# A retention and two routed layers: the state's product in 64x64 parts, tile shapes grouped, first and small slots in another order

## Chip, cores and metric

One core of a Trainium2 chip runs the whole program. The metric is the device time of one launch in microseconds; the time before is the median of three runs. Lower is better.

## What is computed

The reference, cut to what matters (B = 4, H = 8, S = 768, D = 64; N = B S = 3072 tokens of 512 elements; 8 experts, F = 1024):

```python
for t in range(S):                                  # retention
    state = gamma * state + einsum('bhd,bhe->bhde', k[:, :, t], v[:, :, t])
    y[:, :, t] = scale * einsum('bhd,bhde->bhe', q[:, :, t], state)
x = y.transpose(0, 2, 1, 3).reshape(B * S, H * D)
# layer 1: one expert per token
logits = x @ w_gate + modality_bias[modality_id]
e = argmax(logits); gate_w = softmax(logits)[e]
x[mask_e] = gate_w * (relu(x[mask_e] @ w1[e]) @ w2[e])
# layer 2: the same without the bias, and times sigmoid(x @ w_output_gate)[e]
```

All is in 32-bit floats. The layers' products split each operand into a high and a low part (names ending in h and l, as w1h and w1l), of which three products are summed.

## The kernel before

**Retention** (0 to 154.6 us). A unit is one batch's chunk of 128 tokens with all eight heads: 24 units, six chunks for each of four batches. For a unit, q and k, with a decay put on by POOL (`scale`: sq, sv), are turned to have the head's elements on partitions (`tr`: four 128x128 transposes, ACT copies the result to qT or kT), then come the scores q k (`scores`, L651, in two banks, heads of odd and even number apart), which DVE masks into P (L655), and `attend`: the state's product Z q (L664, block diagonal Z of two heads, 128x128, only where the chunk isn't a batch's first) and the values' product P sv (L669) are summed in one bank, from which ACT copies yT (L671). `update` adds k sv to the state (L681, in po[0]); DVE copies one half of it to Z (L684), ACT the other (L685), into tiles whose other blocks POOL zeroed once.

One unit later `rows` turns yT back (L577) so that a row holds a token, and computes the routing's partial products with the gate's weights wgp in four 32-column tiles (L581; DVE copies them to yl, L583); `logits` sums these (L587). Groups of tokens then go through `choose` (L183 to L207, with an exponential rex on ACT, L197), `rank` (L215 and L217, matmuls that count tokens of each expert), `place` and `weigh`; a token's row is then scattered to its expert's block of x1d by an indirect DMA on POOL. Rows that nobody fills are `blank`ed by copies of zeros on SP's queue, in units 3 to 6. After unit 17 `decide` names the first expert, whose weights are fetched behind it.

**Layers.** The rows of an expert are worked through in slots: 256 rows (`run`) or, for the rest, up to 128 (`run_small`). A slot fetches rows (xqb), turns them on DVE (`xpose`, L540), splits them (`xsplit`: xh on ACT L545, xl on DVE L547), multiplies with w1 (L892 or the same in `mm1s`), applies relu and splits (hh, hl), and multiplies with w2 (L910). `split1` and `split2` make the high halves of w1 and w2 on ACT (L505, L510) and the low ones on POOL or DVE (L506, L511). While a slot runs, the layer's outputs (ob) are turned and routed for the next layer (`route`, oT, `tr`, `lgm`, `rank`), at steps listed in BIG_AT, SMALL_AT and FIRST_AT. Layer 1 ends at about 499 us, layer 2 at about 835.

**What sets the order.** Each engine runs its instructions in the order in which the program is written; no scheduler moves them. PE, DVE, ACT, POOL and SP wait for one another by semaphores, so an instruction that waits holds up all behind it on its engine. In the retention the loop over units writes the order: fetch, scale, transposes of the next unit's k, scores, transposes of the next q, rows and logits of the last unit, attend, update, and the lists `early` and `late` of routing steps before and behind attend.

## Time and profile before

| | us |
|---|---|
| median of three runs | 842.93 (841.94 to 845.92) |
| the profiled execution | 841.21 |
| its span | 839.4 |
| PE busy in the span | 796.4 (95%) |
| DVE, ACT, POOL busy | 430.2, 276.4, 192.5 |

The mean granted clock of TensorE is 0.994 of its full rate. The durations below come from the profiled execution: a row gives the start, the busy time, the engine, the line and the tiles, and in brackets for how long the engine had stood idle and what released it. Busy times of neighbours on PE overlap, so the length of a block is the difference of two starts.

### The profile page before, as it was taken

The page shows a single profiled execution, that of the slowest core. Times are in us where ns is not written, and L with a number is a line of the kernel's source. Part 1 is how long each engine was busy: PE and PEld are TensorE (multiplying, and loading weights), DVE is VectorE, ACT ScalarE, POOL GpSimd, SP SyncE. Part 2 cuts the span into 40 slices and gives each one's busy share as a digit, 9 for nine tenths or more (in the row PEclk, how much of TensorE's full clock was granted, in tenths as well). Part 3 has the DMA queues.
Part 4 walks back from the last instruction along what each step waited for, and adds up shares of the span by engine and source line. Part 5 has one row for each costly group of instructions (what it writes and reads, how often), then busy time and mean ns, then how long its engine had stood idle before and what let it go on. Part 6 is the DMA issues. An engine that isn't in the chain of part 4 may idle for free. (4 is left out here: it accounts for less than half of the span.)

```text
span 839.4 us, 18443 instructions
## 1 busy us (share of the span) xinstructions
PE 796.4 (95%) x5987; PEld 691.8 (82%) x5987; DVE 430.2 (51%) x1110; ACT 276.4 (33%) x476; POOL 192.5 (23%) x291
## 2 busy tenths in 40 slices
PE   8999998899999997999999968989999999999996
PEld 8788877878899876888998757887899799999794
DVE  4544565754443338444443586223736485463762
ACT  3444445411221216212212532112424362332641
POOL 3455464811110012111001214011111111011111
PEclk9999999999999999999999999999999999999999
DMA  9988799464111124411221531622636277171531
GB/s 168 229 229 195 161 234 264 176 205 119 37 49 28 39 55 144 139 46 37 74 51 42 167 127 29 232 62 53 189 95 210 75 244 237 51 236 45 183 103 40
DMA packets 149688, 106.98 MB, mean 127 GB/s; under 512 B 94845, under 2 KB 125693, under 8 KB 149504
## 3 DMA queue, kind: packets, MB, share of 16 engines
q1 hardware_dynamic: 141664, 85.37, 38.0%
q0 software_dynamic: 6400, 18.98, 6.1%
q8 instruction: 73, 1.20, 0.6%
q14 instruction: 111, 0.91, 0.4%
q10 hardware_dynamic: 1440, 0.53, 0.3%
HBM read 167.64 MB, written 25.83 MB: 230 GB/s over the span
## 5 line engine op out<-in xcount | busy, mean ns | idle before, releaser
L892 PE MATMUL hT<-xh,w1h 128*128 128x256 f32 x768 | 221.2, 288 | 5.2 <-ACT xh L545 3.0
L892 PE MATMUL hT<-xl,w1h 128*128 128x256 f32 x768 | 215.5, 281 | 2.7 <-DVE xl L547 2.0
L892 PE MATMUL hT<-xh,w1l 128*128 128x256 f32 x768 | 215.0, 280 | 0.0
L910 PE MATMUL po<-w2h,hh 128*128 128x512 f32 x432 | 172.3, 399 | 0.3
L910 PE MATMUL po<-w2l,hh 128*128 128x512 f32 x432 | 171.2, 396 | 0.0
L892 PEld LDWEIGHTS hT<-xh,w1h 128*128 128x128 f32 x768 | 144.9, 189 | 14.0 <-issue 7.6
L892 PEld LDWEIGHTS hT<-xl,w1h 128*128 128x128 f32 x768 | 145.1, 189 | 4.7 <-DVE xl L547 3.2
L892 PEld LDWEIGHTS hT<-xh,w1l 128*128 128x128 f32 x768 | 144.8, 188 | 0.0
L910 PE MATMUL po<-w2h,hl 128*128 128x512 f32 x432 | 136.4, 397 | 1.6 <-DVE hl L884 1.1
L884 DVE SCALAR_TENSOR_TENSOR hl<-hT,hh 128x512 fp32r<-128x512 f32 x96 | 65.2, 689 | 129.6 <-ACT hh L883 99.2
L883 ACT ACTIVATE hh<-hT 128x512 fp32r<-128x512 f32 x96 | 57.0, 597 | 192.9 <-PE hT L892 171.9
L910 PEld LDWEIGHTS po<-w2h,hl 128*128 128x128 f32 x432 | 81.0, 188 | 23.1 <-DVE hl L905 2.0
L910 PEld LDWEIGHTS po<-w2h,hh 128*128 128x128 f32 x432 | 81.4, 188 | 19.7 <-ACT hh L904 1.6
L910 PEld LDWEIGHTS po<-w2l,hh 128*128 128x128 f32 x432 | 81.4, 188 | 18.1
L469 POOL DMA_INDIRECT x2d<-ob,r_idx x28 | 29.6, 1057 | 243.4 <-DVE ob L260 105.2
L920 POOL DMA_INDIRECT out_dram<-ob,to x28 | 29.9, 1069 | 187.0 <-DVE ob L918 135.6
L545 ACT ACTIVATE xh<-xTb 128x512 fp32r<-128x512 f32 x58 | 33.5, 624 | 99.3 <-DVE xTb L540 87.7
L511 DVE TENSOR_TENSOR w2l<-raw,w2h 128x1024 fp32r<-128x1024 f32 x40 | 47.3, 1233 | 14.2 <-DMA xqb<-x1d 6.7
L506 DVE TENSOR_TENSOR w1l<-raw,w1h 128x512 fp32r<-128x512 f32 x80 | 49.8, 684 | 2.5 <-ACT w1h L505 2.5
L547 DVE TENSOR_TENSOR xl<-xTb,xh 128x512 fp32r<-128x512 f32 x58 | 37.5, 688 | 22.3 <-ACT xh L545 22.3
L540 DVE STREAM_TRANSPOSE xTb<-xqb 128x1024 f32<-128x1024 f32 x29 | 36.0, 1242 | 24.4 <-DMA xmb<-x2d 13.4
L505 ACT ACTIVATE w1h<-raw 128x512 fp32r<-128x512 f32 (+1 forms) x84 | 47.7, 640 | 0.0
(205 smaller groups left out, 969.0 us busy)
## 6 DMA issues: line engine op xcount, KB each, us to landing
raw<-in_w_dram SPq DMA_DIRECT2D x248, 512.0 KB
xqb<-x2d SPq DMA_DIRECT2D x124, 64.0 KB
xqb<-x1d SPq DMA_DIRECT2D x108, 64.0 KB
nq<-in_q_dram SPq DMA_DIRECT2D x24, 256.0 KB
nk<-in_k_dram SPq DMA_DIRECT2D x24, 256.0 KB
nv<-in_v_dram SPq DMA_DIRECT2D x24, 256.0 KB
x1d<-zrow SPq DMA_DIRECT2D x4, 516.0 KB
x2d<-zrow SPq DMA_DIRECT2D x4, 516.0 KB
```

The lines of the kernel that those rows point to most:

```text
L469: return nc.gpsimd.indirect_dma_start(out=dst, out_offset=bass.IndirectOffsetOnAxis(ap=rp.idx[:, t:t + 1], axis=0), in_=row, in_offset=Non ...
L505: nc.scalar.activation(w1h[i][:, cols], raw1[i][:, cols], AF.Copy)
L506: los[i].tensor_tensor(w1l[i][:, cols], raw1[i][:, cols], w1h[i][:, cols], op=ALU.subtract)
L511: los[i].tensor_tensor(w2l[i], raw2[i], w2h[i], op=ALU.subtract)
L540: nc.vector.transpose(xT.rearrange("p k (a i) -> p a k i", i=32), xq.rearrange("p a (k i) -> p a k i", k=KD))
L545: nc.scalar.activation(hi[:, k:k + 2, :], xT[:, k:k + 2, :], AF.Copy)
L547: nc.vector.tensor_tensor(lo[:, k:k + 2, :], xT[:, k:k + 2, :], hi[:, k:k + 2, :], op=ALU.subtract)
L883: nc.scalar.activation(hh[b], hT[b], AF.Relu)
L884: nc.vector.scalar_tensor_tensor(hl[b], in0=hT[b], scalar=0.0, in1=hh[b], op0=ALU.max, op1=ALU.subtract)
L892: nc.tensor.matmul(to, lhsT=a[k][:, fs], rhs=b[:, k, :], start=(k == 0 and m == 0), stop=(k == KD - 1 and m == 2))
L910: nc.tensor.matmul(po[h], lhsT=x[b][:, o:o + P], rhs=w[f // 2][:, f % 2, :], start=(f == 0 and i == 0), stop=(f == KF - 1 and x is hl))
L920: nc.gpsimd.indirect_dma_start(out=out, out_offset=bass.IndirectOffsetOnAxis(ap=to[:, t:t + 1], axis=0), in_=o[:, :DM], in_offset=None, bo ...
```

## The change

1. `attend` multiplies with the state in eight 64x64 products instead of four block-diagonal 128x128 ones. The output lies in two banks (hT[3] and xT), the halves of which ACT and DVE copy to yT. Z is one 128x256 tile that DVE copies alone; POOL's zeroed tiles are gone. `rows` permutes its transposes to match, and the gate's weights are loaded in four parts on ACT's queue.
2. In the loop over units products of one tile shape stand together: scores, routing parts (now `parts`, in 128 columns of the bank of the small results), transposes of the next q, rows, transposes of the next k (in the scores' first bank), logits, the routing steps, attend, update. The `late` steps stand before attend. w1's low half is made by DVE, not POOL, behind update in units 20 to 22.
3. The blank rows are written in unit 22, behind the first expert's weights, and no scatter waits for them.
4. In a layer's first slot DVE makes all of w2's low half, at other steps; in small slots of layer 1 each step of split2 stands one later, split1's second half stands behind the output, and SMALL_AT has later steps.

The diff, cut to its core:

```diff
-            if i == 1:
-                rows(0)
-            elif 1 < i < n - 1:
-                tr(i + 1, "kT", "k")
             scores(i)
-            if i == 1:
-                tr(2, "kT", "k", po[1])
+            mask(i, 0)
+            if i:
+                parts(i - 1)
+            mask(i, 1)
             if 0 < i < n - 1:
                 tr(i + 1, "qT", "sq")
-            if i > 1:
+            if i:
                 rows(i - 1)
+            if 0 < i < n - 1:
+                tr(i + 1, "kT", "k", pS[0])
+            if i:
+                logits(i - 1)
             if i == n - 1:
                 xsplit(xh, xl, xTf, "h")
-            if n - 4 <= i < n - 1:
-                split1([nc.gpsimd] * KD, [i - n + 4] if i < n - 2 else [2, 3])
-            if 2 < i < 7:
-                blanks.append(blank(x1d, 2 * i - 6))
-                if i == 6:
-                    blanks.append(blank0(x1d))
+            if i == n - 2:
+                blanks.extend([blank(x1d, e) for e in range(0, E, 2)] + [blank0(x1d)])
             for f in early.get(i, []):
                 f()
+            run(*[f() for f in late.get(i, [])])
-            attend(i, lambda: logits(i - 1) if i else None)
+            attend(i)
             update(i)
+            if n - 4 <= i < n - 1:
+                split1([nc.vector] * KD, [i - n + 4] if i < n - 2 else [2, 3])
-            run(*[f() for f in late.get(i, [])])
...
             if c:
+                for s in range(2):
+                    for r in range(2):
+                        for h in range(2):
+                            o = slice(r * D, r * D + D)
+                            nc.tensor.matmul(py[r][h * D:(h + 1) * D, s, :], lhsT=st["Z"][o, 2 * h + s, :], rhs=d["qT"][o, 2 * h + s, :],
+                                             start=(s == 0), stop=False, skip_group_check=True)
...
-            nc.scalar.activation(yT[i % 2], py, AF.Copy)
+                if r:
+                    nc.vector.tensor_copy(yT[i % 2][:, 2:], py[r])
+                else:
+                    nc.scalar.activation(yT[i % 2][:, :2], py[r], AF.Copy)
...
-                        split2([nc.gpsimd] * 2 + [nc.vector] * 2, ({0: (2, 0, 1), 1: (3,)}, {1: (2, 0), 2: (1, 3)})[self.li - 1].get(f, ()))
+                        split2([nc.vector] * 4, ({0: (0,), 3: (1,), 5: (2,), 7: (3,)}, {1: (0,), 2: (1,), 5: (2,), 7: (3,)})[self.li - 1].get(f, ()))
...
-                self.split2((0,) if self.li == 1 else (0, 1), los)
+                if self.li == 2:
+                    self.split2((0, 1), los)
-                        self.split2((((1,), (2, 3), ()), ((), (2,), (3,)))[self.li - 1][j - 1], los)
+                        self.split2((((0,), (1,), (2, 3)), ((), (2,), (3,)))[self.li - 1][j - 1], los)
-                        self.split1(1)
                 self.done(1)
+                self.split1(1)
-        BIG_AT, SMALL_AT, FIRST_AT = (1, 3, 4, 7, 7, 16, 1), (1, 2, 3, 4, 4, 8, 0), (1, 2, 4, 6, 6, 8, 0)
+        BIG_AT, SMALL_AT, FIRST_AT = (1, 3, 4, 7, 7, 16, 1), (1, 2, 4, 6, 6, 8, 0), (1, 2, 4, 6, 6, 8, 0)
```

What the change moves on PE in a steady unit. Before, from the last of the eight scores, which the transposes of the next k (L638, nk) stand ahead of, to the values' product:

```order
L651 MATMUL hT2_118<-qT_1066,kT_1048 128x128
L638 MATMUL hT0_116<-ident_68,sq_1040 128x128 x4
L577 MATMUL po1_121<-ident_68,yT0_136 128x128 x4
L581 MATMUL xT_122<-yT0_136,wgp_74 32x128 x4
L664 MATMUL hT3_119<-qT_1066,Z0_138 128x128 x4
L587 MATMUL misc_123<-cst_67,yl0_137 128x8
L669 MATMUL hT3_119<-P0_1130,sv_954 64x128
L669 MATMUL hT3_119<-P1_1132,sv_954 64x128
```

After, the same part of a unit:

```order
L652 MATMUL hT2_118<-qT_1321,kT_1332 128x128
L585 MATMUL misc_123<-yT1_124,wgp_74 32x128 x4
L639 MATMUL hT0_116<-ident_68,sq_1296 128x128 x4
L578 MATMUL po1_121<-ident_68,yT1_124 128x2x64 x4
L639 MATMUL hT1_117<-ident_68,nk_1214 128x128 x4
L591 MATMUL misc_123<-cst_67,yl1_125 128x8
L671 MATMUL hT3_119<-qT_1321,Z_1378 64x128 x2
L671 MATMUL xT_122<-qT_1321,Z_1378 64x128 x2
L671 MATMUL hT3_119<-qT_1321,Z_1378 64x128 x2
L671 MATMUL xT_122<-qT_1321,Z_1378 64x128 x2
L676 MATMUL hT3_119<-P0_1401,sv_1222 64x128 x4
L676 MATMUL xT_122<-P1_1408,sv_1222 64x128 x4
```

The transposes of k moved from before the scores to between rows and logits, the routing parts to just behind the scores, and the logits out of the attention; the state's product has eight rows of 64 columns in place of four of 128.

On DVE at the end of the retention (units 21 to 23), before, from the copy of logits and the transposition of the first slot's rows (L540) to the last unit's masks (L655):

```order
L588 COPY r1_lg_238<-misc_123 128x8
L540 STREAM_TRANSPOSE xTf_110<-xqf_108 128x8x4x32
L684 COPY Z0_138<-po0_120 64x4x64
L183 TENSOR_TENSOR r1_lg_238<-r1_lg_238,bias_76 128x16
L186 TENSOR_REDUCE rmx_1_624<-r1_lg_238 128x2
L190 TENSOR_TENSOR rdz_1_627<-r1_lg_238,rmx_1_624 128x16
L201 SCALAR_TENSOR_TENSOR rq_1_635<-rdz_1_627,cst_67 128x16
L205 TENSOR_REDUCE rm2_1_638<-rq_1_635 128x2
L207 TENSOR_TENSOR r1_oh_239<-rq_1_635,rm2_1_638 128x16
L655 TENSOR_TENSOR P0_2063<-hT1_117,cst_67 128x512
L655 TENSOR_TENSOR P1_2065<-hT2_118,cst_67 128x512
```

After:

```order
L201 SCALAR_TENSOR_TENSOR rq_1_625<-rdz_1_617,cst_67 128x16
L205 TENSOR_REDUCE rm2_1_628<-rq_1_625 128x2
L207 TENSOR_TENSOR r1_oh_238<-rq_1_625,rm2_1_628 128x16
L679 COPY yT0_136<-xT_122 128x256
L540 STREAM_TRANSPOSE xTf_110<-xqf_108 128x8x4x32
L694 COPY Z_2138<-po0_120 128x256
L506 TENSOR_TENSOR w1l2_98<-raw12_86,w1h2_94 128x1024
L506 TENSOR_TENSOR w1l3_99<-raw13_87,w1h3_95 128x1024
L657 TENSOR_TENSOR P0_2161<-hT1_117,cst_67 128x512
L587 COPY yl0_137<-misc_123 128x128
L657 TENSOR_TENSOR P1_2168<-hT2_118,cst_67 128x512
```

The choice now stands ahead of the copies of yT and Z, and two w1l stand between Z and the masks.

On DVE in a small slot of layer 1, before, from its start (the branches are the ends of conditional parts; lT and r2_lg are routing results):

```order
L511 TENSOR_TENSOR w2l0_104<-raw20_88,w2h0_100 128x1024
L928 UNCONDITIONAL_BRANCH x2
L928 COMPARE_AND_BRANCH
L511 TENSOR_TENSOR w2l1_105<-raw21_89,w2h1_101 128x1024
L928 UNCONDITIONAL_BRANCH x2
L948 COPY lT2_2161<-misc_123 128x256
L928 COMPARE_AND_BRANCH
L511 TENSOR_TENSOR w2l2_106<-raw22_90,w2h2_102 128x1024
L511 TENSOR_TENSOR w2l3_107<-raw23_91,w2h3_103 128x1024
L928 UNCONDITIONAL_BRANCH x2
L905 TENSOR_TENSOR hl0_2147<-hT2_118,hh0_2143 128x512
L955 COPY r2_lg_2125<-misc_123 128x32
```

After:

```order
L511 TENSOR_TENSOR w2l0_104<-raw20_88,w2h0_100 128x1024
L939 UNCONDITIONAL_BRANCH x2
L959 COPY lT2_2264<-misc_123 128x256
L939 COMPARE_AND_BRANCH
L511 TENSOR_TENSOR w2l1_105<-raw21_89,w2h1_101 128x1024
L939 UNCONDITIONAL_BRANCH x2
L916 TENSOR_TENSOR hl0_2250<-hT2_118,hh0_2246 128x512
L939 COMPARE_AND_BRANCH
L511 TENSOR_TENSOR w2l2_106<-raw22_90,w2h2_102 128x1024
L511 TENSOR_TENSOR w2l3_107<-raw23_91,w2h3_103 128x1024
L939 UNCONDITIONAL_BRANCH x2
L966 COPY r2_lg_2228<-misc_123 128x32
```

The copy lT now stands ahead of the second w2l, and hl ahead of the last two.

## Rows read from the trace of the kernel before

**Rows 1.** Windows: stretch, length, busy of PE, PEld, DVE, ACT, POOL, clock, DMA share, GB/s.
```profile
14.60:154.60 140.00, 129.32 (x1718) 110.41 (x1714) 76.71 (x229) 63.86 (x120) 73.94 (x67) 1.00 0.92 222
...
475.00:528.00 53.00, 42.08 (x247) 34.34 (x246) 35.34 (x130) 20.07 (x33) 12.79 (x11) 0.97 0.36 111
528.00:839.40 311.40, 298.78 (x1808) 260.98 (x1808) 158.03 (x213) 108.35 (x174) 43.10 (x91) 0.99 0.43 136
```
**Rows 2.** Timeline of PE in unit 10: start, busy us, line, operation, tiles.
```profile
67.21 0.64 PE L681 MATMUL po<-sv,nk 128*64 128x64 f32 x16
67.78 0.66 PE L638 MATMUL hT<-ident,nk 128*128 128x128 f32 x4
68.36 1.16 PE L651 MATMUL hT<-qT,kT 64*128 64x128 f32 x16
69.56 0.63 PE L638 MATMUL hT<-ident,sq 128*128 128x128 f32 x4
70.02 0.60 PE L577 MATMUL po<-ident,yT 128*128 128x128 f32 x4
70.55 0.42 PE L581 MATMUL xT<-yT,wgp 128*32 128x128 f32 x8
70.91 1.16 PE L664 MATMUL hT<-qT,Z 128*128 128x128 f32 x8
71.90 0.29 PE L587 MATMUL misc<-cst,yl 128*128 128x8 f32 x2
72.12 1.09 PE L669 MATMUL hT<-P,sv 128*64 128x128 f32 x16
73.04 0.58 PE L681 MATMUL po<-sv,nk 128*64 128x64 f32 x14
```
**Rows 3.** PE by line, 14.6 to 154.6: count, busy, mean ns, idle before, releasers.
```profile
L638 PE MATMUL hT<-ident,sq 128*128 128x128 f32 x88 | 13.9, 280 | 7.8 <-ACT kT L644 4.5 <-ACT rex L197 2.3 <-POOL sq L631 0.6
```
**Rows 4.** Timeline of unit 9, ACT's exponential and PE's transposes of q.
```profile
62.61 0.23 ACT L197 ACTIVATE rex<-rdz 128x32 f32<-128x32 f32 x1 [0.68 <-DVE rdz L190]
...
63.60 0.41 PE L638 MATMUL hT<-ident,sq 128*128 128x128 f32 x2 [0.94 <-ACT kT L644]
```
**Rows 5.** Timeline of unit 21: POOL, DVE, PE.
```profile
133.21 2.35 POOL L506 TENSOR_TENSOR w1l<-raw,w1h 128x1024 fp32r<-128x1024 f32 x1
133.45 2.15 DVE L183 TENSOR_TENSOR r_lg<-r_lg,bias 128x32 f32<-128x32 f32 x1
...
135.85 0.19 DVE L190 TENSOR_TENSOR rdz<-r_lg,rmx 128x32 f32<-128x32 f32 x1
...
136.84 1.05 POOL L631 TENSOR_TENSOR sq<-nq,cst 128x512 f32<-128x512 f32 x1 [1.28 <-DMA nq<-in_q_dram]
...
137.08 0.63 PE L638 MATMUL hT<-ident,sq 128*128 128x128 f32 x4 [2.40 <-ACT kT L644]
```
**Rows 6.** Timeline of the retention's end: DVE's rdz, PE's ranks, the layer's second product.
```profile
148.51 2.07 DVE L190 TENSOR_TENSOR rdz<-r_lg,rmx 128x16 f32<-128x16 f32 x1
...
151.25 0.17 PE L215 MATMUL misc<-r_oh,cb 128*128 128x16 bf16 x1 [2.06 <-DVE r_oh L207]
...
154.99 0.42 PE L892 MATMUL hT<-xl,w1h 128*128 128x256 f32 x1
```
**Rows 7.** Timeline of the change of layers: DVE's w2l, PE's ranks, the next layer's first product.
```profile
482.65 2.36 DVE L511 TENSOR_TENSOR w2l<-raw,w2h 128x1024 fp32r<-128x1024 f32 x2 [6.70 <-DMA xqb<-x1d]
485.27 2.35 DVE L511 TENSOR_TENSOR w2l<-raw,w2h 128x1024 fp32r<-128x1024 f32 x2
...
490.08 0.17 PE L215 MATMUL misc<-r_oh,cb 128*128 128x16 bf16 x1 [2.57 <-DVE r_oh L210]
...
499.75 0.36 PE L892 MATMUL hT<-xh,w1h 128*128 128x256 f32 x1 [1.73 <-ACT w1h L505]
```
**Rows 8.** Timeline of slot 0: PE at hl, DVE's transposition, PE at its end.
```profile
175.07 0.74 PE L910 MATMUL po<-w2h,hl 128*128 128x512 f32 x2 [1.09 <-DVE hl L884]
...
179.76 1.25 DVE L540 STREAM_TRANSPOSE xTb<-xqb 128x1024 f32<-128x1024 f32 x1 [3.16 <-DMA xmb<-x1d]
...
181.78 0.38 PE L892 MATMUL hT<-xh,w1h 128*128 128x256 f32 x1 [0.38 <-ACT xh L545]
182.51 0.38 PE L892 MATMUL hT<-xl,w1h 128*128 128x256 f32 x1 [0.34 <-DVE xl L547]
```
**Rows 9.** Timeline of a small slot in layer 1: PE's transposes of the output.
```profile
329.87 0.66 PE L940 MATMUL xT<-ident,ob 128*128 128x128 f32 x4 [1.05 <-ACT oT L941]
```

More of the change, by code (lines that the diff above doesn't have):

```diff
@@ L592, in scatter1 @@
         ins = scatter(x1d, rp1, t, yn[t // 4 % 2][:, t % 4, :])
-        for o in scattered[-1:] if scattered else blanks:
+        for o in scattered[-1:] + blanks:
             tc.declare_no_dep(ins, o, reason="every row has a place of its own")
@@ L606, in retention_moe_moe_kernel @@
         yT[0], yl[0] = ak.tile([P, 4, P], F32, name="yT0", bufs=1), ak.tile([P, P], F32, name="yl0", bufs=1)
-        pT, pS, pyT, pU = hT[0], hT[1:3], hT[3], po[0]
-        zs = [ak.tile([P, 4, P], F32, name=f"Z{i}", bufs=1) for i in range(2)]
-        for z in zs:
-            nc.gpsimd.memset(z, 0.0)
+        pT, pS, pyT, pU = hT[0], hT[1:3], (hT[3], xT), po[0]
         units = [(b, c) for b in range(B) for c in range(NCH)]
@@ L682, in update @@
                                      start=(c == 0 and j == 0), stop=True, skip_group_check=True)
-            Z = zs[i % 2]
-            nc.vector.tensor_copy(Z[0:D, :, 0:D], U[0:D])
-            nc.scalar.activation(Z[D:P, :, D:P], U[D:P], AF.Copy)
-            st["Z"] = Z
+            st["Z"] = ak.tile([P, 4, D], F32, name="Z")
+            nc.vector.tensor_copy(st["Z"], U)
         idle = xTf[:, 0, 0:P // 2]
@@ L702, in retention_moe_moe_kernel @@
         nc.vector.memset(wgp, 0.0)
-        nc.sync.dma_start(wgp[:, :, 0:E], wg.rearrange("p (k e) -> p k e", k=KD))
+        for h in range(2):
+            for r in range(2):
+                nc.scalar.dma_start(wgp[h * D:(h + 1) * D, 2 * r:2 * r + 2, 0:E], wg[r * D:(r + 1) * D, :].rearrange("p (h s e) -> p h s e", h=2, s=2)[:, h])
         fetch(1)
@@ L709, in retention_moe_moe_kernel @@
         warm(1)
-        tr(0, "kT", "k", pyT, halves=True)
+        tr(0, "kT", "k", pyT[0], halves=True)
         warm(2)
@@ L1145, in retention_moe_moe_kernel @@
         last = NT1 - 1
-        first(1, [(1, [lambda: rows(last)]), (2, [lambda: logits(last), g1["choose"], blank2]), (5, [g1["rank"]])], g1, 5,
+        first(1, [(1, [lambda: parts(last), lambda: rows(last)]), (2, [lambda: logits(last), g1["choose"], blank2]), (5, [g1["rank"]])], g1, 5,
               lambda: [scatter1(t) for t in range(NT1 - 2, NT1)])
```

35 lines of the change are left out of this document (17 added, 18 removed).

## The prediction

> **What bounds the kernel now.** I read the busy time by stage first [rows 1]. TensorE (PE) is busy for 129.3 of the 140.0 us of the retention that run in steady order, for 42.1 of the 53 us around the change of layers, and for 298.8 of the last 311.4 us. So the last 311 us hold 12.6 us of idle PE, of which little can be had; the gain must come from PE's work in the retention, from its waits there, and from the stretch around 475 to 528. Then I read PE's timeline over one undisturbed unit, number 10 [rows 2]: update 0.57, transposes of k 0.58, scores 1.20, transposes of q 0.46, rows 0.53, routing parts 0.36, state's product 0.91 to 0.99, logits 0.22, values' product 0.92, together 5.83 us from one update to the next (differences of the starts). Inside a block of full 128x128 products one starts every 0.11 us (four transposes take 0.44 to 0.46); where the next block has another tile shape, some 0.1 us is added (0.58 for the four transposes of k against 0.46 for those of q, which are followed by a block of their own shape). Last I read PE's waits grouped by line, which say what ended each idle time [rows 3], and three places behind them [rows 4 to 6].
>
> **The state's product** (20 of 24 units have one). Before: four products, each in two passes, eight instructions at 0.11 and a change of shape, 0.99. After: eight products in 64x64 parts, sixteen instructions. What that costs depends on how many parts run at once, which no row shows for 64x64. Bounds: one at a time 16 x 0.11 + 0.1 = 1.85, a loss of 0.86 a unit; two at a time, as the values' product does in its 128x64 parts (16 instructions in 0.92), 0.97, no gain; four at a time, as the routing parts do in their 128x32 tiles (8 instructions in 0.36), 4 x 0.11 + 0.1 = 0.55, a gain of 0.44. I take four: each quarter of the array shares its rows with one other quarter and its columns with one, the two diagonal pairs share nothing, and the nearest row with four tiles, the routing parts, runs them so. 20 x 0.43 = **8.6**. [...]
>
> **Groups of one tiling together** (23 units). Six changes of shape in a unit become five; the transposes of k stand between other 128x128 blocks (0.58 to 0.44), rows too (0.53 to 0.44), and the scores no longer wait some 0.1 for the copy of kT just made: 23 x 0.34 = **7.8**. In the three later units that open a batch the logits no longer cut the values' product in two: +0.3 each, **0.9**. The unit then takes 5.83 - 0.44 - 0.34 = 5.05.
>
> **Waits in the retention.** The 88 transposes of q waited 7.8 us in all, 4.5 for kT's copy and 2.3 for the exponential [rows 3]. The reason stands in unit 9: ACT's exponential waited for DVE's rdz, the copy of kT stood behind it, and PE waited 0.94 for that [rows 4]. In unit 21 it was 2.40, since DVE's L183 took 2.15 (0.19 for the like operation L190 behind it) while POOL's w1l of 2.35 ran [rows 5]. The choice now stands behind the unit's copies, so 6.8 of this goes. What is late next: the ranks' matmul waits for the logits' copy and shares the bank with it, some 0.45 x 6 groups = -2.7; the expert's choice in unit 17 with its successor, -1.4 (one DVE chain as in [rows 4], twice); the four w1l now on DVE take it 1.2 each, the price of w2l there [rows 7], in the gap that DVE has in a unit (76.7 busy of 140, [rows 1]), -1.0 for what sticks out. Net **+1.7**. [...]
>
> **End of the retention.** Before: rdz takes 2.07 beside POOL, ranks' matmul waits 2.06 for the choice, and the layer's second product stands at 154.99 [rows 6]. After: no POOL work slows DVE, but DVE gets the transposition (1.25), two w1l (2.4), the last group's choice and place, all ahead of the masks and xl. I set **-1.7** (between +2, the wait of 2.06 gone, and -4, the two w1l and the transposition wholly on the path). Blank rows (4 x 516 KB) go from units 3 to 6 to unit 22 behind the weights on SP's queue: nothing cost in the middle, since no row waits for them before the second slot; if the queue has not run dry by then, the first slot's rows come later. The four issues of the gate's weights on ACT at the start lie beside waiting for loads: 0.
>
> Retention: 8.6 + 7.8 + 0.9 + 1.7 - 1.7 = **17.3**.
>
> **Slots.** Slot 0 lost 1.09 at hl and 0.38 + 0.34 at its end, where the transposition waited 3.16 for rows [rows 8]. With the splits on DVE, one each at f = 0, 3, 5, 7, the last stands at the same place: the wait at hl stays; the end wait goes if the rows come earlier. **+0.7**. In small slots the first w2l leave DVE's head, and with them what keeps the copies of the output; PE's wait of 1.05 for oT [rows 9] shrinks, **+0.8**. At the change of layers DVE stood for 6.70 until rows were there and then had w2l four times in two pairs of 2.36 ahead of everything [rows 7]; the ranks' matmul waited 2.57, the next layer's first product 1.73. Later w2l clear DVE's start; the later split1 puts w1's low half behind the output. Between 2 (one of the two waits) and 6 (both, and 1.7 of the same queue): **+4.5**. Layer 2 has all its splits moved by a step at most: 0.
>
> **Sum:** 17.3 + 0.7 + 0.8 + 4.5 = 23.3 against the profiled 841.2, so 817.9. The median of three, 842.9, is 1.7 above the profiled time; predicted for it: 819.5.
>
> **Rivals.**
> (a) *64x64 parts run two at a time.* For it: in the values' product neighbours in the row pair up, and all four write two banks only. The 8.6 fall away: 828.
> (b) *Loads bound the shorter retention.* The 140 us moved 222 GB/s at a share of 0.92 [rows 1], so full is 241; 31.1 MB at that are 129 us, a saving of 11 where I count 17.3; sq already waited 1.28 for its load in unit 21 [rows 5], and 2 MB of blanks now fall there too. Against it: weights for layer 1 (2 MB of w2) and blanks may land behind the retention's end, which makes the floor 112 to 120. With half the gain at the change of layers: 828. The same time comes out if the end of the retention, bound by DVE, loses the -4.
> (c) *Slower: each 64x64 product drains the array.* If every change of bank and quarter costs what a change of shape does (0.2 apiece), the sixteen take 3.2 instead of 0.99, +2.2 in 20 units = 44, less the other 15 of the sum: 871. It turns slower when the state's product takes more than 0.99 + 15 / 20 = 1.7 a unit. Against it: scores alternate two banks and two row halves at 0.11 a pair [rows 2].
> (d) *The order does nothing*, because another wait of the same length takes the place of each that went and only the mode changes come: (a) and (b) together, some 838 to 842.
>
> **How the numbers follow.** Forecast 0.62, (a) 0.16, (b) 0.15, (d) 0.03, (c) 0.04. The range 811 to 831 holds the forecast with its bounds (end of retention +2 to -4, change of layers 2 to 6, waits +4 to -1) and (a) and (b). Beyond 0.5% of 842.9, that is 4.2 us, about what a measurement can tell from no change, faster has 0.62 + 0.16 + 0.15 = 0.93, same 0.03, slower 0.04.
>
> **What would show it.** In the changed profile: state's product starts to values' product starts 0.55 (right), 0.97 (a), over 1.7 (c); a steady unit of 5.05 from update to update; transposes of k at 0.44; no wait of PE for kT behind the exponential; first product of layer 1 near 137; DVE's w1l of 1.2 in units 20 to 22 with no POOL work beside them stretched; a wait of PE for nq or k would be (b). The forecast is wrong if the units stay above 5.4 or if the change of layers keeps its 2.57 and 1.73.

## The result and the profile after

The changed kernel takes 826.8 us in the median (823.34 to 829.31), the kernel before in the same session 843.23 (841.94 to 845.92): a ratio of 0.983 with a 95% interval of 0.980 to 0.986. Faster by 1.7%, 16.4 us, where 23.4 of gain and 819.5 us had been forecast, with a range of 811 to 831. The profiled execution took 823.34 with a span of 821.5; against the 841.21 and 839.4 before, that is 17.9 us, and the points below are told in those two executions. The mean granted clock is 0.994 in the one and 0.987 in the other.

PE's timeline over unit 10 of the changed kernel (start, busy us, line, tiles), the answer to [rows 2]:

```profile
62.88 1.16 PE L652 MATMUL hT<-qT,kT 64*128 64x128 f32 x16
...
64.82 0.60 PE L578 MATMUL po<-ident,yT 128*128 128x128 f32 x4
65.26 0.60 PE L639 MATMUL hT<-ident,nk 128*128 128x128 f32 x4
65.69 0.29 PE L591 MATMUL misc<-cst,yl 128*128 128x8 f32 x2
65.91 0.33 PE L671 MATMUL hT<-qT,Z 64*64 64x128 f32 x2
65.92 0.33 PE L671 MATMUL xT<-qT,Z 64*64 64x128 f32 x2
66.07 0.28 PE L671 MATMUL hT<-qT,Z 64*64 64x128 f32 x2
66.08 0.28 PE L671 MATMUL xT<-qT,Z 64*64 64x128 f32 x2
...
66.51 0.66 PE L676 MATMUL hT<-P,sv 128*64 128x128 f32 x8
...
68.00 0.60 PE L652 MATMUL hT<-qT,kT 64*128 64x128 f32 x6
```

From scores to scores a unit takes 68.00 - 62.88 = 5.12 us, before 5.83. The state's product takes 66.51 - 65.91 = 0.60 in place of 0.99: the rows start in pairs 0.01 apart, each row holds two instructions, and the eight rows of the sixteen instructions start in four pairs, so four quarters of the array do run at once. The transposes of k take 0.43 (before 0.58), rows 0.44 (0.53). So the steady unit is what was forecast (5.05) but for 0.07.

Where the time went, stage by stage (minus is time gained; the forecast is split by the prediction's own terms). At the scores of unit 2 the kernel before has already done the transposes of k for unit 3, the changed one not, so that some 0.5 us of work lies on the other side of that line:

| | before | after | moved by | forecast |
|---|---|---|---|---|
| scores of unit 2 start | 20.08 | 20.81 | +0.7 | -0.8 |
| scores of unit 23 start | 147.08 | 133.15 | -14.7 more | -17.5 |
| second product of layer 1 | 154.99 | 142.84 | +1.8 more, -12.2 in all | +0.9 (1.7 less unit 23's own gain), -17.3 in all |
| through slot 0 and the start of slot 1 | | | -1.9 | -0.7 |
| through the small slot in layer 1 | | | -1.6 | -0.8 |
| through the change of layers, to layer 2's first product with w2 | 516.16 | 495.61 | -4.9 | -4.5 |
| layer 2 | | | +2.6 | 0 |

PE's waits by line in the retention, 14.6 to 142 (count, busy us, mean ns, idle before, releasers), the answer to [rows 3]:

```profile
L639 PE MATMUL hT<-ident,sq 128*128 128x128 f32 x88 | 14.9, 293 | 1.5 <-POOL sq L632 1.5
L639 PE MATMUL hT<-ident,nk 128*128 128x128 f32 x88 | 13.8, 281 | 0.6 <-DVE P L657 0.6
L585 PE MATMUL misc<-yT,wgp 128*32 128x128 f32 x176 | 10.9, 285 | 2.9 <-DVE yT L679 2.9
L591 PE MATMUL misc<-cst,yl 128*128 128x8 f32 x46 | 6.8, 221 | 2.6 <-DVE yl L587 2.6
L215 PE MATMUL misc<-r_oh,cb 128*128 128x32 bf16 (+1 forms) x6 | 1.1, 175 | 1.6 <-DVE r_lg L592 1.6
```

The old wait for kT behind the exponential is gone from the list. In its place stand waits for three copies by DVE. Unit 13 shows how the largest comes about (timeline of POOL, DVE and PE):

```profile
76.60 1.06 POOL L632 TENSOR_TENSOR sq<-nq,cst 128x512 f32<-128x512 f32 x1
...
76.67 2.04 DVE L201 SCALAR_TENSOR_TENSOR rq<-rdz,cst 128x32 f32<-128x32 f32 x1
...
77.60 1.05 POOL L632 TENSOR_TENSOR sv<-nv,cst 128x512 f32<-128x512 f32 x1
...
79.07 0.42 DVE L679 COPY yT<-xT 128x256 f32<-128x256 f32 x1
...
79.55 0.41 PE L585 MATMUL misc<-yT,wgp 128*32 128x128 f32 x4 [0.87 <-DVE yT L679]
```

DVE's L201 (0.19 for a like operation in [rows 5]) lasted for as long as POOL's two scalings ran, and the copy of yT's second half, which the change had given to DVE, stood behind that chain. The times agree: L201 ran from 76.67 to 78.71, POOL's two from 76.60 to 78.65. What makes DVE's operation longer beside POOL isn't shown.

The end of the retention (timeline of DVE and PE), the answer to [rows 6]; the two w1l stand between Z and the last masks, and PE waits behind them:

```profile
133.18 1.25 DVE L540 STREAM_TRANSPOSE xTf<-xqf 128x1024 f32<-128x1024 f32 x1
...
134.66 2.34 DVE L506 TENSOR_TENSOR w1l<-raw,w1h 128x1024 fp32r<-128x1024 f32 x2
...
137.86 0.39 PE L591 MATMUL misc<-cst,yl 128*128 128x8 f32 x2 [2.60 <-DVE yl L587]
...
142.84 0.38 PE L903 MATMUL hT<-xl,w1h 128*128 128x256 f32 x1 [0.76 <-DVE xl L547]
```

In slot 0 and at the change of layers (timeline of PE; the answers to [rows 8] and [rows 7]) PE now waits for the last w2l, and for the choice in the last slot of layer 1 1.21 in place of 2.57, for w1h 0.42 in place of 1.73:

```profile
161.62 0.50 PE L921 MATMUL po<-w2l,hh 128*128 128x512 f32 x1 [1.62 <-DVE w2l L511]
```

```profile
472.25 0.17 PE L215 MATMUL misc<-r_oh,cb 128*128 128x16 bf16 x1 [1.21 <-DVE r_oh L210]
...
480.12 0.36 PE L903 MATMUL hT<-xh,w1h 128*128 128x256 f32 x1 [0.42 <-ACT w1h L505]
...
492.61 0.18 PE L215 MATMUL misc<-r_oh,cb 128*128 128x16 bf16 x1
```

The last row is the ranks' matmul in layer 2's first slot, which waits for nothing. In the kernel before it did wait (timeline of PE), which [rows 7] doesn't hold:

```profile
513.20 0.17 PE L215 MATMUL misc<-r_oh,cb 128*128 128x16 bf16 x1 [2.58 <-DVE r_oh L210]
```

And the clock. Windows of PE (stretch, length, PE busy, granted clock, DMA share, GB/s), first the changed kernel, then the one before:

```profile
15.00:19.00 4.00, 3.38 (x22) 0.57 0.85 100
138.00:142.00 4.00, 3.72 (x38) 0.57 1.02 364
476.00:480.00 4.00, 3.62 (x8) 0.57 0.31 116
510.00:518.00 8.00, 5.47 (x27) 0.57 0.99 362
```

```profile
153.00:157.00 4.00, 4.00 (x29) 0.57 0.54 203
491.00:495.00 4.00, 4.00 (x14) 0.57 0.22 83
```

In windows of 0.4 us the clock is 0.50 within such a stretch and 1.00 around it (15.8 to 18.6 in the first), so 0.57 over 4 us is some 3.4 us at 0.50 and the rest at 1.00. Ahead of layer 2's middle the changed kernel has 17 us at the lower level, the one before 6.8; every such stretch comes after PE has started nothing for some us (1.8 at 13.8, 2.9 at 135.0, 1.6 twice at 471 to 474, 1.8 at 507.6 with another 2.7 from 510.4 on), though not every standstill has one behind it (none after 2.5 at 307). What it costs can be read in the state's product of the last unit: 1.06 us in place of 0.60. These two executions overstate the difference, though: of the kernel before, 44 more executions stand on record beside the runs below, with granted clocks of 0.981 to 0.998 and a median of 0.988, so that the profiled one with 0.994 is among the highest; the changed kernel's four have 0.983 to 0.987. By the medians (0.988 and 0.9855) the changed kernel has some 4 us more at 0.50, an estimate from these figures, worth 2 us at most.

### The profile page after: what moved, and what is told of

It is laid out like the page before. It is cut to its first block, busy times and chain, and to the rows that moved or that the text cites. A ratio compares the mean times of both kernels' runs of the same rounds, so it can differ in the third digit from the quotient of the medians.

```text
span 821.5 us, 18747 instructions
## 1 busy us (share of the span) xinstructions
PE 785.4 (96%) x6147; PEld 684.4 (83%) x6147; DVE 440.0 (54%) x1142; ACT 261.5 (32%) x456; POOL 175.4 (21%) x281
## 5 line engine op out<-in xcount | busy, mean ns | idle before, releaser
L511 DVE TENSOR_TENSOR w2l<-raw,w2h 128x1024 fp32r<-128x1024 f32 x44 | 51.8, 1221 | 9.7 <-ACT hs L1064 4.5
L506 DVE TENSOR_TENSOR w1l<-raw,w1h 128x512 fp32r<-128x512 f32 (+1 forms) x84 | 54.6, 711 | 2.7 <-ACT w1h L505 2.6
L540 DVE STREAM_TRANSPOSE xTb<-xqb 128x1024 f32<-128x1024 f32 x29 | 36.1, 1243 | 22.4 <-DMA xmb<-x2d 8.6
```

Of the source, the lines that this page charges most:

```text
L506: los[i].tensor_tensor(w1l[i][:, cols], raw1[i][:, cols], w1h[i][:, cols], op=ALU.subtract)
L511: los[i].tensor_tensor(w2l[i], raw2[i], w2h[i], op=ALU.subtract)
L540: nc.vector.transpose(xT.rearrange("p k (a i) -> p a k i", i=32), xq.rearrange("p a (k i) -> p a k i", k=KD))
```

## The experiments

All times are medians, and ratios go against the kernel before on the same chip in the same session. The changed kernel's is 0.983 (0.980 to 0.986). The runs stand in several sessions, so small differences between them are read by the ratios; one of 4 us or less lies within the intervals, and there the traces have to decide.

| run | us | ratio (95%) |
|---|---|---|
| after, old state's product | 833.1 | 0.991 (0.988 to 0.995) |
| before, 64x64 product alone | 853.0 | 1.013 (1.009 to 1.018) |
| the same, logits between the products | 846.1 | 1.004 (1.001 to 1.007) |
| after, late steps behind update | 834.5 | 0.993 (0.990 to 0.996) |
| after, yT copied by ACT | 822.9 | 0.981 (0.977 to 0.985) |
| after, w1l on POOL | 827.4 | 0.983 (0.980 to 0.987) |
| yT by ACT, end of retention reordered | 825.4 | 0.981 (0.978 to 0.985) |
| after, products in two waits | 828.1 | 0.985 (0.981 to 0.988) |
| after, first slots' w2 split as before | 836.7 | 0.994 (0.992 to 0.996) |
| after, small slots as before | 827.9 | 0.984 (0.981 to 0.988) |
| after, no load in layer 2's first slot | 823.4 | 0.979 (0.975 to 0.982) |
| yT by ACT, first slots' w2 split earlier | 822.6 | 0.977 (0.972 to 0.981) |

**The state's product undone.** `attend`, `update`, `rows` and the layout of the gate's weights of the kernel before, in the new order:

```diff
...
-                            nc.tensor.matmul(py[r][h * D:(h + 1) * D, s, :], lhsT=st["Z"][o, 2 * h + s, :], rhs=d["qT"][o, 2 * h + s, :],
-                                             start=(s == 0), stop=False, skip_group_check=True)
...
+                for j in range(4):
+                    nc.tensor.matmul(py[:, j, :], lhsT=st["Z"][:, j, :], rhs=d["qT"][:, j, :], start=(j == 0), stop=False, skip_group_check=True)
...
```

> The changed kernel with the state's product as before (four block-diagonal 128x128 products, one output bank, ACT's copy of yT, Z in two halves), everything else changed. Theory (four 64x64 parts run at once, 0.60 a unit against 0.99, and PE sets the unit): a steady unit goes from 5.12 back to 5.52, 20 units x 0.40 = 8 us, so 834 to 836. Rival (the units are bound by loads or by DVE, and the shorter product only makes PE wait longer): less than 4 us slower than the changed kernel, below 831.

Measured: 833.1, and a unit of 5.51 as forecast (5.52):

```profile
64.05 1.16 PE L654 MATMUL hT<-qT,kT 64*128 64x128 f32 x16
...
67.01 1.14 PE L668 MATMUL hT<-qT,Z 128*128 128x128 f32 x8
68.07 1.09 PE L671 MATMUL hT<-P,sv 128*64 128x128 f32 x16
...
69.56 0.71 PE L654 MATMUL hT<-qT,kT 64*128 64x128 f32 x7
```

By the ratios the product is worth 0.8%, 6.7 us, and in the two traces the way from the scores of unit 2 to those of unit 23 is 6.7 us longer here (119.0 against 112.3). The theory holds, with 1 us less than its 8. It also gives the grouping by itself: 5.83 - 5.51 = 0.32 a unit.

**The product alone, in the kernel before.**

```diff
         def attend(i, between):
+            between()
...
+                            nc.tensor.matmul(py[r][h * D:(h + 1) * D, s, :], lhsT=st["Z"][o, 2 * h + s, :], rhs=d["qT"][o, 2 * h + s, :],
+                                             start=(s == 0), stop=False, skip_group_check=True)
...
```

> The kernel before with the state's product in 64x64 parts alone (with the layout of yT and the gate's weights that go with it; logits stand just before it). Theory: the same 0.40 a unit, 20 x 0.40 = 8 us of 843, so 835, with the kernel's old waits (7.8 us before the transposes of q) unchanged. Rival (the parts gain only where products of one tiling stand together): 840 or more.

Measured: 853.0, slower than the kernel before by 1.3%. The product took 0.60 here too. PE's waits by line show what it had covered (first the kernel before, 14.6 to 154.6, then this run, 14.6 to 165):

```profile
L587 PE MATMUL misc<-cst,yl 128*128 128x8 f32 x46 | 7.1, 227 | 0.6 <-DVE yl L583 0.3 <-DVE rR L221 0.3
```

```profile
L588 PE MATMUL misc<-cst,yl 128*128 128x8 f32 x46 | 8.8, 264 | 9.9 <-DVE yl L584 8.2 <-DVE rR L221 1.7
```

The logits need yl, which DVE copies right behind the masks; the old place of the state's product, 0.99 us between parts and logits, had hidden that copy. Neither theory nor rival had this. It isn't the whole loss: of the 12.4 us that this trace is longer, 7.2 are there at layer 1's second product, and 7.4 come in layer 2's first slot, whose code is the old one (31.6 us to the next slot's w2 products, before 24.2; see the run without the load), while the stretches between give some back. With the logits put back between the two products:

```diff
         def attend(i, between):
-            between()
...
+            between()
             for r in range(2):
                 for s in range(2):
```

> As the run with the 64x64 product alone in the kernel before, but with the logits left between the state's and the values' product, where they stood. In the first such run the product took 0.60 as forecast, but PE waited 0.57 a unit for the routing parts' copy yl, which the longer product had covered. Theory (what covers the copy decides): the wait shrinks to about 0.1 to 0.2, unit 5.83 - 0.40 + 0.1 = 5.5, total 835 to 838. Rival (the shorter product in the old order only moves the wait, here to the 64x64 product's own cover): 840 or more.

Measured: 846.1, no gain, the rival's figure. The steady unit is 5.46 as the theory said, 0.37 shorter, but where a batch begins there is no state's product to cover anything, and PE waited 1.44 for yl, with DVE's routing chain ahead of it:

```profile
45.06 1.02 DVE L241 CAST yn<-rrm 128x4 f32<-128x4 uint32 x1
...
47.52 0.39 PE L588 MATMUL misc<-cst,yl 128*128 128x8 f32 x2 [1.44 <-DVE yl L584]
```

Unit 6 took 7.96 and unit 18 8.26 (before 5.07 and 5.50), and the clock fell to its lower level after each (3.4 us at 0.50 each, from 47 and from 119 on); the ranks' matmul waited 6.4 for yl in all, before 2.1 for the choice. At layer 1's second product this trace is 2.5 us behind the kernel before; another 7.0 come in layer 2's first slot, which the edit doesn't touch. In the kernel before, the values' product was split round the logits there; this run hasn't that, so it undoes a little more than it means to. What follows: in the old order the shorter product is no gain, in the new one, in which qT, rows and kT stand between the parts and the logits, it is.

**The late routing steps behind update.**

```diff
-            run(*[f() for f in late.get(i, [])])
             if i == 0:
                 fetch(3)
...
+            run(*[f() for f in late.get(i, [])])
             for t in written.get(i, []):
```

> The changed kernel with the late routing steps (choose, place, weigh, decide) behind update, where the kernel before had them. Theory (it is their place ahead of yT's second copy on DVE that makes the routing parts wait): PE's waits ahead of the parts in units 6, 13 and 18 go as they did with the copy on ACT, 3 to 4 us, 823 to 824; the old wait for kT's copy behind the exponential doesn't come back, since kT is now copied before the exponential. Rival (choose then ends too late for the ranks of the next unit, or the masks wait behind it): as much is lost there, 826 to 828.

Measured: 834.5, 8 us slower than the changed kernel; theory and rival had both put it lower. PE's waits by line:

```profile
L639 PE MATMUL hT<-ident,nk 128*128 128x128 f32 x88 | 13.8, 279 | 8.4 <-DVE P L657 6.3 <-DVE r_oh L207 2.0
...
L585 PE MATMUL misc<-yT,wgp 128*32 128x128 f32 x176 | 9.8, 285 | 1.0 <-DVE yT L679 1.0
```

The parts' wait did shrink (2.9 to 1.0), and that for the exponential didn't return. But the transposes of k now write into the scores' first bank, so they wait until DVE has masked it, and the chain now stood ahead of the mask: 8.4 us. So the place of the late steps ahead of attend is a part of the gain that cannot be left out of this change.

**yT copied by ACT.**

```diff
-                if r:
-                    nc.vector.tensor_copy(yT[i % 2][:, 2:], py[r])
-                else:
-                    nc.scalar.activation(yT[i % 2][:, :2], py[r], AF.Copy)
+                nc.scalar.activation(yT[i % 2][:, 2 * r:2 * r + 2], py[r], AF.Copy)
```

> The changed kernel with both halves of yT copied by ACT. Theory (the new wait of the routing parts, 0.65 in unit 6, 1.1 in 13 and 1.9 in 18, is the copy of yT's second half queued on DVE behind choose and decide): these three waits go, 3 us, so 822 to 824. Rival (the chain on DVE delays the masks and yl anyway): PE waits for these instead, under 1 us gained, 826.

Measured: 822.9, in the theory's range. The parts no longer wait:

```profile
L585 PE MATMUL misc<-yT,wgp 128*32 128x128 f32 x183 | 9.8, 285 | 0.0
```

Some of it is found again as 1.7 at the transposes of k (masks; 0.6 in the changed kernel) and 3.6 at yl in the last unit (2.6). The ratio's interval overlaps that of the changed kernel; the traces are what decides. Units 6, 13 and 18, which had waited, take 15.8 us together in place of 18.7. The two other runs with ACT's copies take 15.6 and 16.3, the five that have the changed kernel's code in these units 17.5 to 20.3, so this is more than they spread.

**w1's low half on POOL.**

```diff
-                split1([nc.vector] * KD, [i - n + 4] if i < n - 2 else [2, 3])
+                split1([nc.gpsimd] * KD, [i - n + 4] if i < n - 2 else [2, 3])
```

> The changed kernel with w1's low half for the first slot made by POOL again, at the same place. Theory (the two w1l of 1.2 each on DVE ahead of the last unit's masks and yl make PE wait 2.6 there, and the clock falls to its half level for 3.4 us after it): that wait and the lower clock go, 3 to 4.5 us, first product of layer 1 near 138 instead of 141.6. Rival (POOL's work slows DVE's operations beside it, as rdz with 2.07 in the kernel before, and holds up the scatters): a wait of 2 us at the ranks returns and less than 1 us is gained.

Measured: 827.4, no gain. Timeline of POOL, DVE and PE:

```profile
133.07 4.68 POOL L506 TENSOR_TENSOR w1l<-raw,w1h 128x1024 fp32r<-128x1024 f32 x2 [2.85 <-ACT w1h L505]
...
134.35 1.25 DVE L540 STREAM_TRANSPOSE xTf<-xqf 128x1024 f32<-128x1024 f32 x1 [1.88 <-DMA xqf<-x1d]
...
169.32 0.39 PE L903 MATMUL hT<-xh,w1h 128*128 128x256 f32 x1 [3.03 <-ACT xh L545]
```

The layer's second product came 8.0 us after the last unit's scores in place of 9.7, a part of what the theory had. But PE's wait for yl only went from 2.60 to 2.26: DVE, free of w1l, waited 1.88 for the first slot's rows. And POOL's scatters came 4 us later, so that the next slot's rows were late and PE waited 3.03 there; slot 1's products with w2 come 3.9 us later after those scores than in the changed kernel. The rival's result, for a reason it hadn't named in full.

**The end of the retention in another order on DVE** (with yT on ACT): Z, masks and yl of the last unit, then the transposition and the two w1l, the last places behind xl.

```diff
...
-            run(*[f() for f in late.get(i, [])])
+            if i == n - 1:
+                xpose(xTf, xqf)
+                xsplit(xh, xl, xTf, "h")
+                for m in (2, 3):
+                    nc.vector.tensor_tensor(w1l[m], raw1[m], w1h[m], op=ALU.subtract)
+            else:
+                run(*[f() for f in late.get(i, [])])
...
```

> The run with ACT's copies of yT, and at the end of the retention DVE does Z, masks and yl of the last unit first, then the first slot's transposition and the two w1l, and the last group's places behind xl. Theory (DVE's order at the end makes the 3.8 us that PE waits for yl, 1.6 of them for rows of the first slot at the head of its queue): PE's wait for yl goes, the layer's second product 2 us earlier than in that run, 820 to 821. Rival (DVE's work as a whole, not its order, sets the end): PE waits for xl in place of yl, 822 to 823.

Measured: 825.4, no gain over the run it builds on. The wait for yl is gone, and two others stand for it, on PE:

```profile
136.53 0.38 PE L907 MATMUL hT<-xh,w1h 128*128 128x256 f32 x1 [0.77 <-ACT xh L545]
138.71 0.38 PE L907 MATMUL hT<-xl,w1h 128*128 128x256 f32 x1 [1.80 <-DVE xl L547]
```

The second product comes 7.7 us after the last unit's scores, in the run it builds on 9.3; by slot 1's products with w2 nothing of that is left (50.2 us against 50.0). That fits the rival, by which DVE's work there as a whole is the bound and not its order; the time is above the rival's 822 to 823.

**Products in the waits.**

```diff
+            if i == 1:
+                for _ in range(28):
+                    nc.tensor.matmul(small_bank[:, 0:P], lhsT=idle, rhs=idle, start=True, stop=True)
...
+            if i == n - 1:
+                for _ in range(46):
+                    nc.tensor.matmul(small_bank[:, 0:P], lhsT=cb[:, P:2 * P], rhs=cb[:, P:2 * P], start=True, stop=True)
             if i:
                 logits(i - 1)
```

> The changed kernel with products that nobody reads on PE in two waits: 28 of 128x128 in bf16 ahead of the transposes of q in unit 1, 46 ahead of the logits in the last unit. Theory (after those waits PE's clock is at its half level for 3.4 us each, and products in the wait keep it up): the clock stays at its upper level there, the last unit's products and the first of layer 1 take 0.6 and 0.92 again, 1.5 to 3 us gained, 824 to 825. Rival (DVE and the loads set the end of the retention whatever the clock is): PE's faster products wait for xl, within 1 us, 826 to 827.

Measured: 828.1, and the test failed in what it was to test. The products stand in the bank of small results, which yl was still to be read from, and so they waited for the very copy that they were to bridge:

```profile
139.92 4.22 PE L762 MATMUL misc<-cb 128*128 128x128 bf16 x46 [3.63 <-DVE yl L587]
```

They then ran at the lower clock (0.50 from 140 to 143) and came on top. In unit 1 the clock stayed up (1.00) behind the 28 products, but it did so without them too in eight other runs with the same start, and the scores of unit 3 come no sooner (25.74, there 25.50 to 26.31). What a higher clock in the last unit would give stays open.

**The first slots' w2 split as before.**

```diff
-                        split2([nc.vector] * 4, ({0: (0,), 3: (1,), 5: (2,), 7: (3,)}, {1: (0,), 2: (1,), 5: (2,), 7: (3,)})[self.li - 1].get(f, ()))
+                        split2([nc.gpsimd] * 2 + [nc.vector] * 2, ({0: (2, 0, 1), 1: (3,)}, {1: (2, 0), 2: (1, 3)})[self.li - 1].get(f, ()))
```

> The changed kernel with w2's low half of a layer's first slot made as before (two parts on POOL, two on DVE, at its start). Theory (on DVE at the slot's later steps the last part stands behind the chain that plans the slots, and PE waits for it, 2.0 in layer 1 and 1.1 in layer 2): slot 0 gets 2.0 back but for POOL's contention with DVE, which cost 1.5 before, so 826 to 828, no change. Rival (POOL's splits were the cheaper): 823 to 824.

Measured: 836.7, 9 to 10 us slower than the changed kernel, against both expectations. From the w2 products of a slot in layer 1's middle (364.9 before) to layer 2's first it took 151.6 us (after 146.4, before 151.2): all of the gain at the change of layers goes with this one line. Eight traces that have the changed kernel's code there take 146.2 to 147.5, so this is more than they spread. Timeline there, in layer 2's first slot:

```profile
497.96 5.68 POOL L511 TENSOR_TENSOR w2l<-raw,w2h 128x1024 fp32r<-128x1024 f32 x2 [0.24 <-PE misc L964]
498.44 3.01 DVE L511 TENSOR_TENSOR w2l<-raw,w2h 128x1024 fp32r<-128x1024 f32 x1 [1.28 <-ACT w2h L510]
...
502.39 1.29 DVE L190 TENSOR_TENSOR rdz<-r_lg,rmx 128x16 f32<-128x16 f32 x1
...
504.64 0.17 PE L215 MATMUL misc<-r_oh,cb 128*128 128x16 bf16 x1 [3.81 <-DVE r_oh L210]
```

With POOL at work beside it DVE's w2l took 3.01 (1.22 alone) and rdz 1.29 (0.17); the choice was late, and PE waited 3.81 for it, where the kernel before waited 2.58 and the changed one not at all. Another 4 us lie in slot 0 and around it (from the last unit's scores to slot 1's product with w2 52.9 us, after 48.8); there this trace has 10.2 us at the lower clock, the changed kernel's 3.4, and how much of the 4 is the edit's isn't shown.

**The small slots as before.**

```diff
-                if self.li == 2:
-                    self.split2((0, 1), los)
+                self.split2((0,) if self.li == 1 else (0, 1), los)
...
-                        self.split2((((0,), (1,), (2, 3)), ((), (2,), (3,)))[self.li - 1][j - 1], los)
+                        self.split2((((1,), (2, 3), ()), ((), (2,), (3,)))[self.li - 1][j - 1], los)
...
```

> The changed kernel with the small slots' order as before (w2l one step earlier in layer 1, w1's second half ahead of the output, the old steps of the routing). Theory (this order made the 5.0 us gained around the change of layers and 1.9 at the small slot in layer 1): 5 to 7 us slower than the changed kernel, 832 to 834. Rival (that gain came from the layer reaching its end earlier against the loads): within 2 us, 825 to 829.

Measured: 827.9, 1 us slower, the rival's figure. The same stretch round the change of layers took 147.9 in place of 146.4: this part makes 1.5 of the 4.9 at most, for the eight traces named above reach 147.5, and this one has 6.8 us more at the lower clock there. Between slot 1 and the small slot's w2 products it is 0.9 slower (143.4, after 142.6), of the 1.6 gained there.

**No load in layer 2's first slot.** In the changed kernel the next expert's weights are loaded there. PE's row behind them:

```profile
513.10 0.58 PE L903 MATMUL hT<-xh,w1h 128*128 128x256 f32 x1 [2.39 <-issue]
```

```diff
-                        self.load(raw1, w1)
-                        self.load(raw2, w2)
+                        if self.li == 1:
+                            self.load(raw1, w1)
+                            self.load(raw2, w2)
```

> The changed kernel with the load of the next expert's weights (8 DMAs of 512 KB) left out in layer 2's first slot, so that later slots use old weights there. In the changed kernel PE stood still for 2.4 us at 510 with nothing that the profile shows, beside that load at a DMA share of 0.9 and with instruction packets in the queues, and the clock was then at its half level for 6.8 us; so it was (4.0) in the runs with the 64x64 product alone and with the old split of w2, whose layer 2 is the old one. Theory (PE's instructions come through the same DMA queues and stand behind the weights): without the load the standstill and the lower clock go, second slot of layer 2 at 24 to 25 us in place of 30, total 821 to 823. Rival (a fixed cost of that place of the program): the standstill stays, 826 to 827.

Measured: 823.4, 3 to 4 us less. PE's row at that place:

```profile
512.66 0.38 PE L903 MATMUL hT<-xh,w1h 128*128 128x256 f32 x1 [0.18 <-issue]
```

The standstill is gone, and the lower clock lasts 3.4 us, not 6.8. But that the load causes the standstill is not shown. Ten of the thirteen traces with the load have it, from 2.0 to 4.0 us; the kernel before, the run with the old state's product and the run with products in the waits don't, and the last two have the same layer 2 as the changed kernel. The row at that place in the run with the old product, which follows the one before it by 0.12 us:

```profile
520.88 0.28 PE L895 MATMUL hT<-xh,w1h 128*128 128x256 f32 x1
```

So one trace without load and without standstill can be one more of these, and the intervals of the two ratios (0.979 and 0.983) overlap. That PE's instructions wait in the DMA queues is a guess: from 505 to 516 the changed kernel has four instruction packets, in queues 8 and 14, while 3.04 of the 3.41 MB moved are in queue 1. The second slot is at 28.1 us, not 24 to 25 (27.7 and 26.6 in the two runs that have the load and no standstill). PE waits 1.83 there for the slot's rows, a wait that the kernel before has one slot later (1.93).

**w2 split earlier in the first slots** (with yT on ACT).

```diff
-                        split2([nc.vector] * 4, ({0: (0,), 3: (1,), 5: (2,), 7: (3,)}, {1: (0,), 2: (1,), 5: (2,), 7: (3,)})[self.li - 1].get(f, ()))
+                        split2([nc.vector] * 4, ({0: (0,), 2: (1,), 4: (2,), 6: (3,)}, {1: (0,), 2: (1,), 4: (2,), 6: (3,)})[self.li - 1].get(f, ()))
```

> The run with ACT's copies of yT, and w2's low half in the first slots at f = 0, 2, 4, 6 (layer 1) and 1, 2, 4, 6 (layer 2) in place of 0, 3, 5, 7 and 1, 2, 5, 7. Theory (the last part stood behind the planning chain on DVE): PE's waits for w2l go, 2.1 in slot 0 and 1.1 in layer 2's first, 819.5 to 821. Rival (the chain is then late and with it the fetch of the next slot's rows): PE waits at the next slot's start, 822 to 824.

Measured: 822.6, the lowest median of all, 0.3 under the run it builds on; by the ratios (0.977 and 0.981, of different sessions, with intervals that overlap) it is 3 us, so the times don't tell theory and rival apart. In the trace PE's waits for w2l are gone, and the next slots' starts wait more, 0.66 in layer 1 (there none) and in layer 2 2.58 (there 1.85):

```profile
508.53 0.38 PE L900 MATMUL hT<-xh,w1h 128*128 128x256 f32 x1 [2.58 <-ACT xh L545]
```

From layer 1's second product to slot 1's products with w2 1.0 us is gained (39.6 against 40.7), in layer 2's first slot 0.1 (30.6 against 30.7): mostly the rival's way.

## Why the prediction came out as it did

The time lies in the range, and the direction and the mechanism of the largest terms were right; the sum was 7 us too large in the median, 5.4 in the profiled executions. Of these the retention makes 5.2: 1.5 at its start, 2.8 in its middle (0.5 of it the work across the line named above), 0.9 at its end. Behind it the slots gave 2.4 more than set and layer 2 lost 2.6 where nothing was set, and that these two cancel is luck.

- **The state's product: right.** 0.60 with the change of shape where 0.55 was taken, 0.39 a unit, 7.8 against 8.6. The nearest row, the routing parts with four tiles at once, was the right one to choose. Rivals (a) (0.97) and (c) (over 1.7) are out, and (d), by which the order does nothing, with the time. The 0.2 that (c) puts on every change of bank and quarter was the author's estimate and shows in no row: the product's eight rows start 0.01 to 0.15 apart.
- **Groups of one tiling: right.** 0.32 a unit where 0.34 was taken (0.32 in the run without the new product too), 7.4 against 7.8; the change of shape from the routing parts to the transposes of q costs 0.03 there (they take 0.49, before 0.46). The three units that open a batch gave 0.7 where 0.9 was set (4.52 us against 5.07, less the 0.32).
- **Waits in the retention: the old ones went, one new one was missed.** Net +1.7 had been set. What units 2 to 22 take beyond their undisturbed length (5.83 and 5.12; less for the last and the first unit of a batch) sums to 8.8 before and 8.1 after, so 0.7. Of the three new waits in the list the ranks came out as set (0.5 in units 9 and 17, which have nothing else; 0.45 taken), and so did the w1l (0.8 and 0.2 in units 21 and 22; 1.0 taken); the choice of the first expert cost 2.0 in unit 18 (1.4 taken), as a wait of the parts for yT. What the list did not have is the copy of yT that the change itself had moved into DVE's queue: units 6 and 13 lost 0.8 and 1.3 behind it. The runs with ACT's copies, in which these three units are 2.9 us shorter, bear that out.
- **The start: not thought of.** Units 0 and 1 were to gain 0.8 and lost 0.7. PE reached unit 1 two us sooner, then stood 1.5 for sq, whose load had not landed (POOL's scaling waited 1.91 for it), and ran on at the lower clock for 3.4 us. This is rival (b) in one place; its sign, a wait for loads, shows nowhere else among PE's waits in the retention. The lower clock is this execution's own: in eight runs with the same start PE stood 1.1 to 1.7 in unit 1 and 1.1 to 1.6 again in unit 2, both times for sq and with the clock up, and all reach the scores of unit 3 at 25.5 to 26.3, this one at 25.93 (before 26.52). So the loads set the start, and the lower clock cost nothing there.
- **End of the retention: nearly right.** A loss of 1.7 was set, with the two w1l on the path as said. The stage lost 1.8, but unit 23's own shorter work (0.7) lies in it, so the end cost 2.5. That the other order of DVE gives nothing fits DVE's whole load as the bound.
- **Slots: the change of layers right in size, with the wrong cause.** It gave 4.9 where 4.5 was set, but the prediction put that to the small slots' later w2l. Undone, these cost 1.5 at most. What carries it is the first slots' split on DVE, priced at nothing in layer 2; undone, it takes all of the 4.9. Part of it is a wait of 2.58 at the ranks' matmul in layer 2's first slot, which the prediction had not read. So the right size is luck. Slot 0 and the small slot gave 1.9 and 1.6 where 0.7 and 0.8 were set. The row with DVE held up beside POOL (2.15 for L183 in [rows 5]) had been read for the retention and not carried over to layer 2's first slot, where POOL did the same.
- **Layer 2: 0 set, 2.6 lost.** From the first to the second slot's products with w2 it took 30.3 us in place of 24.2, through a standstill beside a load (2.4), 6.8 us at the lower clock and a wait for rows that the kernel before has one slot later; the next slot gave 2.8 back. The standstill is no cost of the change's idea: runs whose layer 2 is the old one had it (the product alone in the kernel before), and two whose layer 2 is the new one had not. What decides it stays open.

The sum was made of removed work. What it left out is that PE, with work removed, stands longer at places where DVE or a load sets the pace: 1.5 us for sq in unit 1, 2.0 for yT in units 6 and 13, 2.6 for yl in the last unit. The clock adds to it (an estimate of 2 us at most, by the medians above), and no run here tests how much, since the one that was to keep the clock up in the last unit failed.

## What to carry to other kernels

Work that is taken off the bounding engine may be the cover of a copy: look up what stands between a copy and its reader before and after, in the unit that lacks the work too (the 64x64 product alone made the retention 7.2 or 2.5 us longer, by the place of the logits; with the new order the kernel gained 0.8% by it). An order that gains can be a set: here the transposes of k took the scores' bank, and so the routing chain had to stand behind the masks; with the chain at its old place half the gain was lost. The other pieces were not taken out by themselves. When DVE and POOL both have operations in a stretch, price a small one of DVE that others wait for at POOL's length too: here one took 2.04 in place of 0.19, while others beside POOL kept theirs (0.15 for the copy of the logits in the run with w1l on POOL). And before a difference is put down to a stage, look whether other traces of the same code show it there: the start, the standstill in layer 2 and the clock differed between executions of equal code by as much as the terms at issue.

## What the runs showed of the hardware

- 64x64 products on four quarters of the array, with outputs in two banks, start four at a time; sixteen instructions take 0.60 us with the change of shape.
- PE can stand still for 2.0 to 4.0 us beside a load of weights of 4 MB with nothing that it waits for in the profile. It did so in ten of thirteen traces with that load, and not in the one without it; the cause is not shown.
- Some operations of DVE last longer beside POOL: 2.04 us in place of 0.19 beside two of POOL that ran for 2.05, 3.01 in place of 1.22 and 1.29 in place of 0.17 beside two that ran for 5.68. Others don't: the transposition took 1.25 and the masks 0.67 each beside POOL's 4.68 of w1l, as in the changed kernel (1.25 and 0.68).
- The lower clock (0.50) came in stretches of 3.4, 6.8 and, in five runs, 10.2 us, apart from one at each program's end, and only behind a standstill of PE. Which standstill has one behind it is not settled: 2.5 us at 307 had none in the changed kernel, while the run with ACT's copies had 3.4 us of it in that place.
